# Seven half products in place of eight: Strassen's form in the second MLP product of seven blocks

## The chip, the cores and the metric

The kernel runs on one core of a Trainium2 chip. The metric is the device time in microseconds (us) of one execution. One execution is also taken by the hardware profiler; its span runs from the first to the last instruction. PE or TensorE is the matmul engine (PEld its weight loads), DVE is VectorE, ACT is ScalarE, POOL is GpSimd, SP the queue that issues most DMAs. SBUF is the on-chip memory, PSUM the matmul's accumulators in eight banks.

## The reference

Attention over pooled keys and values, then a residual MLP that first mixes tokens and then channels. 8 batches, 8 heads, 576 tokens of 64 elements a head; model width 512, hidden width 2048.

```python
k_p = k.reshape(B, H, Sp, pool, D).mean(axis=3)        # 576 keys -> 72
v_p = v.reshape(B, H, Sp, pool, D).mean(axis=3)
scores = scale * np.matmul(q, k_p.transpose(0, 1, 3, 2))
attn = softmax(scores)
x = matmul(attn, v_p), heads side by side              # 8 x 576 x 512
a1 = alpha1 * x + beta1
tok = np.einsum('ts,bsd->btd', w_tok, a1)
u = x + lam * tok
a2 = alpha2 * u + beta2
ch = np.maximum(a2 @ w_ch1, 0.0) @ w_ch2
out = u + lam * ch                                     # float32
```

## The kernel before, in words

The 8 x 576 = 4608 rows are cut into 36 chunks of 128 rows (the last 64 rows of two batches share one chunk), and four chunks make a block: nine blocks of 512 rows, 0 to 8. Batch 0's attention and token mix come first. Then the loop at the end of the kernel runs over the blocks n = 0 to 8. In each pass it does block n's MLP and, beside it, the attention and token mix of batch n+1 (so in passes 0 to 6), and it starts the loads of batch n+2.

The order within a pass is written by hand: every step is put in the list `todo` with a number, the list is sorted, and the steps are recorded in that order. The numbers count groups of the MLP: 0 to 15 are the first product's sixteen groups, 16 to 31 the second product's. Each engine and each queue works off its own instructions in the order in which they are recorded, and waits for others by semaphores that the tile layer sets. There is no scheduler behind this.

- First product, `mlp_A(n, j)` (L645): four matmuls of 128x512 give one of 16 groups of hidden columns (L651); ScalarE applies bias and Relu from PSUM to a bf16 tile `Hj` (L657). Its input u_fm is the block's u, times alpha2, in bf16, transposed by DMA (`mix_uT`, L625).
- Second product, `mlp_B(n, m, part)` (L662): for each of four chunks m, 16 matmuls of 128x512 that accumulate in one bank (L686). Then VectorE multiplies the bank by lam (L692), adds it to u (L693), and SP stores the chunk (L695, L699). In block 8 w2 is scaled by lam beforehand (`scale_w2`, L368, four operations), and the last chunk is done in two halves of 256 columns (L675, L680, L682).
- Attention of one batch: `sum_k` (L183, L185) pools keys on GpSimd, `att_K` (L439, L445) transposes them on TensorE, `att_S4` (L511, L518) makes the scores of four heads, ScalarE exponentiates (L540), `att_V` (L479, L481) pools values on VectorE in three operations a pair of heads, `att_AV` (L555, L559) multiplies, and VectorE divides by the row sums: a reciprocal (L561) and x_tm (L563). `att_X` (L577) and `rest_X` (L570) scale x_tm to xs for two heads at a time, on VectorE, or on GpSimd for heads 4 and 5.
- Token mix, `mix_T(b, c)` (L609): five matmuls of 128x512 for each chunk c, from number 21 on, so in the midst of the second product. They need xs of all heads. VectorE adds x (L613) and makes u_bf = u * alpha2 in bf16 (L616); `mix_uT` transposes it into the input of a later block.

Banks: six of the eight are handed out from one pool (`gp`), to whatever asks next; two ("ch") serve the scores and the second product.

Of the kernel before, what the change touches and what calls it, by code (L numbers as in the profile page):

```python
# [7 lines left out]
FP = mybir.dt.float32  # L8
F16 = mybir.dt.float16
BF = mybir.dt.bfloat16  # L10
# [13 lines left out]
def kernel(  # L24
# [176 lines left out]
    b2row = const.tile([4, P], FP, tag="b2row", name="b2row")  # L201
# [18 lines left out]
    nc.scalar.dma_start(out=b2row, in_=moe_beta2.rearrange("(c p) -> c p", p=P))  # L220
    warm = const.tile([P, DM], BF, tag="warm", name="warm")
# [7 lines left out]
    vr16 = const.tile([P, H, 1, D], F16, tag="vr16", name="vr16")  # L229
# [81 lines left out]
    def setup_vectors():  # L311
        ps = gp("ps_vec")
        nc.tensor.transpose(out=ps[:, 0:4], in_=b2row, identity=identity[0:4, 0:4])
        nc.scalar.copy(out=b2c_bf, in_=ps[:, 0:4])
        u_fm[0] = work.tile([P, 4, 2, 258], BF, tag="u_fm", bufs=3, name="u_fm")
        nc.scalar.copy(out=u_fm[0][:, :, 0, 256], in_=ps[:, 0:4])
# [39 lines left out]

    def load_w1(g):
# [8 lines left out]

    def scale_w2(g):
        nc.vector.tensor_tensor(  # L368
            out=w2[g], in0=w2[g], in1=lam_bc.unsqueeze(1).to_broadcast((P, 4, DM)), op=ALU.mult)
# [105 lines left out]
    def att_V(b, hp):  # L475

        t = st1[b]["v"][hp // 2][:, 2 * (hp % 2):2 * (hp % 2) + 2]
        for n in (4, 2):
            nc.vector.tensor_tensor(out=t[:, :, 0:n], in0=t[:, :, 0:n], in1=t[:, :, n:2 * n],  # L479
                                    op=ALU.add)  # L480
        nc.vector.tensor_tensor(out=vp1_pool[hp][:, :, 0:64], in0=t[:, :, 0], in1=t[:, :, 1],  # L481
                                op=ALU.add)
# [101 lines left out]
    st2 = {}  # L584
    u_fm = {}

    def chunk_of(b, c):
        key = (b, c) if c < 4 else (b - b % 2, 4)
        if key not in st2:
            st2[key] = {  # L590
                "u": work.tile([P, DM], FP, tag="u_sb", bufs=12, name="u_sb"),
# [10 lines left out]
    def mix_T(b, c, eng=nc.vector):  # L602
# [13 lines left out]
        eng.tensor_tensor(out=s["u_bf"], in0=s["u"], in1=al2_bc, op=ALU.mult)  # L616
# [19 lines left out]
    Hj = {}  # L636
# [3 lines left out]
    def mlp_A(n, j, t0=0, t1=512):  # L640
# [15 lines left out]
        t = work.tile([P, 512], BF, tag="Hj", bufs=18, name="Hj")  # L656
        nc.scalar.activation(out=t, in_=ps_h, func=AF.Relu, bias=bias_cols[:, j:j + 1], scale=1.0)  # L657
        Hj[n, j] = t
# [3 lines left out]
    def mlp_B(n, m, part):  # L662
# [5 lines left out]
        if n == NBLK - 1 and m == 3:  # L668
            half = part // 2
            cols = slice(256 * half, 256 * half + 256)  # L670
            if part == 2:
                ps_ch[m] = gp("ps_ch2")
            ps = ps_ch[m][:, 0:256]
            for j in range(8 * (part % 2), 8 * (part % 2) + 8):
                nc.tensor.matmul(out=ps, lhsT=Hj[n, j][:, 128 * m:128 * m + 128],  # L675
                                 rhs=w2[j // 4][:, j % 4, cols], start=(j == 0), stop=(j == NJ - 1))
            if part % 2:
                b, c = chunks[4 * n + m]
                u = st2[b, c]["u"][:, cols]
                nc.vector.tensor_tensor(out=u, in0=u, in1=ps, op=ALU.add)  # L680
                for i, queue in enumerate((nc.sync, nc.scalar)):
                    queue.dma_start(out=out[b + i, 512:576, cols], in_=u[64 * i:64 * i + 64, :])  # L682
            return
        ps = ps_ch[m]
        for j in range(4 * part, 4 * part + 4):
            nc.tensor.matmul(out=ps, lhsT=Hj[n, j][:, 128 * m:128 * m + 128], rhs=w2[j // 4][:, j % 4, :],  # L686
                             start=(j == 0), stop=(j == NJ - 1))
        if part == 3:
            b, c = chunks[4 * n + m]
            u = st2[b, c]["u"]  # L690
            if n < NBLK - 1:
                nc.vector.tensor_tensor(out=ps, in0=lam_bc, in1=ps, op=ALU.mult)  # L692
            nc.vector.tensor_tensor(out=u, in0=u, in1=ps, op=ALU.add)  # L693
            if c < 4:
                nc.sync.dma_start(  # L695
                    out=out[b, 0:512, :].rearrange("(p c) d -> p c d", c=4)[:, c, :], in_=u)
# [210 lines left out]
```

## Time and profile before

| what | value |
|---|---|
| time, median of 3 runs | 346.75 us (345.08 to 347.48) |
| span of the profiled execution | 342.9 us |
| the median less this span | 3.85 us |
| granted TensorE clock | 1.000 |
| second product, 128x512 (L686), busy | 128.5 us |
| first product, 128x512 (L651), busy | 124.0 us |
| DMA | 45.76 MB, mean 133 GB/s |

The profiled execution is one execution, and its own time is its span and what lies around it; the table gives the distance to the median. "Busy" is the time in which an engine had such an instruction in hand; matmuls overlap in the array, so the time that one costs in a stream is the distance from one to the next, not its mean duration. Behind the bar of a row stands the idle time of the engine ahead of these instructions and what ended it. In the rows in order of time the first number is the start, the second the length, and in brackets stands the idle time just before.

### The profile page before, as it was taken

What the parts mean: (1) busy time and instruction counts of PE and PEld (TensorE: products, weight loads), DVE (VectorE), ACT (ScalarE), POOL (GpSimd) and SP (SyncE); (2) the same over time, 40 slices, a digit from 0 to 9 for tenths busy, and PEclk for the clock granted to TensorE, in tenths of its full rate; (3) what the DMA queues carried; (4) which work ended last, traced back from release to release, by engine and by line L of the source; (5) the groups of instructions that cost most, each with busy time, mean ns of one, the idle gap of its engine ahead of it and who ended that gap; (6) DMA issues with size and microseconds to landing.
All of it is one profiled execution on the core that took longest, in us unless ns stands there. A gap on an engine that the chain in (4) does not pass through costs nothing.

```text
span 342.9 us, 5845 instructions
## 1 busy us (share of the span) xinstructions
PE 333.6 (97%) x2168; PEld 177.2 (52%) x2204; DVE 222.2 (65%) x477; ACT 146.6 (43%) x277; POOL 94.1 (27%) x110
## 2 busy tenths in 40 slices
PE   8999998999999999999999999999999999999995
PEld 2668753455445544555445544554455445545544
DVE  6772468985777678866866698758676881037511
ACT  3667960079106820484038501870088006604700
POOL 8769357201144022701170217002600200000000
PEclk9999999999999999999999999999999999999999
DMA  8999979959788906894599447982800132011012
GB/s 122 192 222 280 267 133 276 182 140 136 159 228 172 175 0 187 160 227 51 175 161 210 62 127 189 180 130 68 243 35 1 48 77 76 2 61 62 2 54 69
DMA packets 66030, 45.76 MB, mean 133 GB/s; under 512 B 34345, under 2 KB 56237, under 8 KB 66002
## 3 DMA queue, kind: packets, MB, share of 16 engines
q1 hardware_dynamic: 51716, 32.73, 40.6%
q0 software_dynamic: 13824, 12.40, 22.6%
q8 instruction: 17, 0.28, 0.3%
q10 hardware_dynamic: 462, 0.27, 0.3%
q14 instruction: 11, 0.09, 0.1%
HBM read 38.30 MB, written 9.44 MB: 139 GB/s over the span
## 4 chain that ended last, share of the span: by engine, by line
PE 91%; DVE 2%; DMA 2%; POOL 2%; issue 1%; POOLq 0%; DVEq 0%
PE ps_h L651 36%; PE ps_ch L686 34%; PE ps_tok L609 11%; PE ps_s L511 2%; PE ps_av L555 2%; DMA q_bf<-in_q_dram 2%; PE ps_ch L675 1%; PE ps_r L518 1%; PE ps_av L559 1%; PE ps_kp L439 1%; PE ps_w L325 0%; PE ps_q L396 0%; DVE ps_ch L692 0%; DVE u_sb L693 0%; DVE u_sb L613 0%
## 5 line engine op out<-in xcount | busy, mean ns | idle before, releaser
L657 ACT ACTIVATE Hj<-ps_h,bias_cols 128x512 bf16<-128x512 f32 x144 | 98.1, 688 | 165.7 <-PE ps_h L651 164.0
L651 PE MATMUL ps_h<-u_fm,w 128*128 128x512 bf16 (+2 forms) x591 | 132.7, 368 | 1.1 <-DVE bias_cols L654 0.2
L686 PE MATMUL ps_ch<-w,Hj 128*128 128x512 bf16 x543 | 128.5, 379 | 0.9 <-issue 0.5
L651 PEld LDWEIGHTS <-w 128*128 128x128 bf16 x608 | 65.5, 114 | 51.2 <-issue 3.0
L686 PEld LDWEIGHTS <-Hj 128*128 128x128 bf16 x560 | 52.9, 98 | 61.6 <-issue 1.6
L609 PE MATMUL ps_tok<-xs,wtT 128*128 128x512 bf16 (+2 forms) x199 | 44.8, 380 | 1.3 <-DVE xs L577 0.9
L577 POOL TENSOR_TENSOR xs<-x_tm,lamal_bc 128x512 bf16<-128x512 f32 x12 | 15.2, 1267 | 106.1 <-DVE x_tm L563 105.9
L692 DVE TENSOR_TENSOR ps_ch<-lam_bc,ps_ch 128x512 f32<-128x512 f32 x32 | 22.1, 692 | 33.5 <-PE ps_ch L686 33.3
L613 DVE TENSOR_TENSOR u_sb<-x_tm,ps_tok 128x512 f32<-128x512 f32 (+1 forms) x40 | 27.3, 683 | 10.9 <-PE ps_tok L609 10.8
L561 DVE RECIPROCAL rec<-ps_av 128x5 f32<-128x5 f32 x64 | 12.2, 191 | 32.7 <-PE ps_av L559 32.4
L563 DVE TENSOR_TENSOR x_tm<-ps_av,rec 128x320 f32<-128x320 f32 x64 | 31.4, 491 | 2.7
L693 DVE TENSOR_TENSOR u_sb<-u_sb,ps_ch 128x512 f32<-128x512 f32 x35 | 24.0, 687 | 13.6 <-PE ps_ch L686 12.5
L540 ACT ACTIVATE ET<-ps_s 72x512 f16<-72x512 f32 x56 | 32.3, 591 | 0.0
L609 PEld LDWEIGHTS <-wtT 128*128 128x128 bf16 (+3 forms) x200 | 17.3, 100 | 22.1 <-issue 1.7
L616 DVE TENSOR_TENSOR u_bf<-u_sb,al_bc 128x512 bf16<-128x512 f32 x34 | 27.1, 798 | 2.2 <-DMA u_fm<-u_bf 1.1
L479 DVE TENSOR_TENSOR v_u<-v_u 72x512 f32<-72x512 f32 (+1 forms) x48 | 26.4, 550 | 0.8
L183 POOL TENSOR_TENSOR k_raw<-k_raw 128x512 f32<-128x512 f32 x14 | 18.4, 1316 | 10.3 <-DMA k_raw<-in_k_dram 10.2
L555 PEld LDWEIGHTS <-ET 72*128 72x128 f16 x256 | 13.9, 97 | 9.3 <-DVE vp L472 0.6
L185 POOL TENSOR_TENSOR k_bf<-k_raw 128x512 bf16<-128x512 f32 x14 | 18.1, 1295 | 1.1
L79 POOL DMA_DIRECT2D q_bf<-in_q_dram x16 | 12.6, 791 | 15.3 <-DVE v_u L158 14.5
L555 PE MATMUL ps_av<-vp,ET 72*128 72x66 f16 x256 | 15.6, 193 | 0.0
L577 DVE TENSOR_TENSOR xs<-x_tm,lamal_bc 128x512 bf16<-128x512 f32 x20 | 14.7, 736 | 0.7
(130 smaller groups left out, 214.3 us busy)
## 6 DMA issues: line engine op xcount, KB each, us to landing
out_dram<-u_sb SPq DMA_DIRECT2D x32, 256.0 KB
k_raw<-in_k_dram SPq DMA_DIRECT2D x12, 512.0 KB
v_u<-in_v_dram SPq DMA_DIRECT2D x12, 512.0 KB
q_bf<-in_q_dram POOLq DMA_DIRECT2D x16, 256.0 KB, 6.3
w<-in_moe_w_ch_dram POOLq DMA_DIRECT2D x6, 512.0 KB, 13.2
w<-in_moe_w_ch_dram POOLq DMA_DIRECT2D x1, 1024.0 KB, 14.8
k_raw<-in_k_dram POOLq DMA_DIRECT2D x2, 512.0 KB, 16.7
v_main<-in_v_dram POOLq DMA_DIRECT2D x1, 1024.0 KB, 12.0
```

Of the source, the lines that this page charges most:

```text
L479: nc.vector.tensor_tensor(out=t[:, :, 0:n], in0=t[:, :, 0:n], in1=t[:, :, n:2 * n], op=ALU.add)
L540: nc.scalar.activation(out=o, in_=i, func=AF.Exp, bias=0.0, scale=0.125)
L555: nc.tensor.matmul(out=av[:, odd + c, :], lhsT=ET[:, m0:m0 + 128], rhs=vp1[:, hh, :])
L563: nc.vector.tensor_tensor(out=x[:, 1 - odd:6 - odd, dd:dd + D], in0=av[:, :, 0:64], in1=rec.unsqueeze(2).to_broadcast((P, 5, D)), op=ALU.mult)
L577: eng.tensor_tensor(out=xs[:, 0:4, cols], in0=x[:, 1:5, cols], in1=lamal_bc[:, cols].unsqueeze(1).to_broadcast((P, 4, D * (h1 - h0))), op= ...
L609: nc.tensor.matmul(out=ps_tok[p0:p1], lhsT=wtT[0:kk, at, P * c:P * c + p1 - p0], rhs=xs_pool[i][0:kk, sc, :], start=(sc == 0), stop=(sc == 4))
L613: nc.vector.tensor_tensor(out=s["u"][p0:p1, :], in0=x[p0:p1, 1 + c if c < 4 else 5 - 5 * i, :], in1=ps_tok[p0:p1, 0:DM], op=ALU.add)
L616: eng.tensor_tensor(out=s["u_bf"], in0=s["u"], in1=al2_bc, op=ALU.mult)
L651: nc.tensor.matmul(out=ps_h[:, t0:t1 + one], lhsT=w1_of(cc, j), rhs=rhs, start=(cc == 0), stop=(cc == 3))
L657: nc.scalar.activation(out=t, in_=ps_h, func=AF.Relu, bias=bias_cols[:, j:j + 1], scale=1.0)
L686: nc.tensor.matmul(out=ps, lhsT=Hj[n, j][:, 128 * m:128 * m + 128], rhs=w2[j // 4][:, j % 4, :], start=(j == 0), stop=(j == NJ - 1))
L693: nc.vector.tensor_tensor(out=u, in0=u, in1=ps, op=ALU.add)
```

## The change

It replaces the second product of blocks 2 to 8 by a Strassen-Winograd form. Rows, hidden columns and output columns are each halved. The eight products of halves become seven, each done for two chunks of rows (`product(n, i, pp)`): eight matmuls of 128x256 with a weight load each, 112 a block where there were 64 of 128x512. Around them:

- `hidden_sum`: four sums (two calls each) of halves of the hidden tiles, 128x1024 bf16, on VectorE. S2 and S3 go to tiles of their own, two overwrite halves of the hidden tiles.
- `weight_sum`: four sums (two calls each) of halves of w2, once, on VectorE: in pass 1 from number 23.2 on, the last in pass 2.
- `gather`: products that belong together accumulate in one bank; ScalarE copies product 1 to P1, VectorE adds banks to u and product 6 to P1, GpSimd adds P1 to three quarters of u (two in block 8, where VectorE adds the third).
- `stores`: a block's four chunks are stored at its end, after the last gathers.
- w2 is scaled by lam in pass 1, three quarters on VectorE and one on GpSimd; the multiplication by lam remains in block 0 alone. Block 1 has the old product with scaled w2.
- The hidden tiles are four of 128x4x512 in place of 16, and the first product's groups are done in the order 0-3, 8-11, 4-7, 12-15 from block 2 on.

Beside that: alpha2 is multiplied into w_ch1 by ScalarE in pass 0 (`scale_w1`, twelve operations; alpha2 comes in columns by one more small load and the transposing matmul of beta2), so for batches 1 to 7 u_bf is a plain copy, on ScalarE. `att_V` is one tensor_reduce. u lies in one tile a block (three buffers) in place of twelve chunk tiles. Batches 3 to 7 space their token mix by 1.15 in place of 1.3. The constants that the new sums' tiles take over were used only before.

```diff
+    nc.sync.dma_start(out=b2row[4:8], in_=moe_alpha2.rearrange("(c p) -> c p", p=P))
...
+    def scale_w1(i, cc):
+        nc.scalar.activation(out=w1[i][:, cc, :], in_=w1[i][:, cc, :], func=AF.Copy, bias=0.0,
+                             scale=al2_cols[:, cc:cc + 1])
...
-        for n in (4, 2):
-            nc.vector.tensor_tensor(out=t[:, :, 0:n], in0=t[:, :, 0:n], in1=t[:, :, n:2 * n],
-                                    op=ALU.add)
-        nc.vector.tensor_tensor(out=vp1_pool[hp][:, :, 0:64], in0=t[:, :, 0], in1=t[:, :, 1],
-                                op=ALU.add)
+            nc.vector.tensor_reduce(out=vp1_pool[hp][:, :, 0:64],
+                                    in_=t.rearrange("g h p d -> g h d p"), op=ALU.add, axis=AX.X)
...
-        eng.tensor_tensor(out=s["u_bf"], in0=s["u"], in1=al2_bc, op=ALU.mult)
+        if b:
+            nc.scalar.copy(out=s["u_bf"], in_=s["u"])
+        else:
+            eng.tensor_tensor(out=s["u_bf"], in0=s["u"], in1=al2_bc, op=ALU.mult)
...
-            if n < NBLK - 1:
+            if n == 0:
                 nc.vector.tensor_tensor(out=ps, in0=lam_bc, in1=ps, op=ALU.mult)
...
+    def weight_sum(i, g):
+        lo, hi = w2[g], w2[g + 2]
...
+        o, a, b = {
+            1: (T1, lo[:, :, HALF:], lo[:, :, 0:HALF]),
+            3: (T3, hi[:, :, HALF:], lo[:, :, HALF:]),
+            2: (T2, hi[:, :, HALF:], T1),
+            4: (T4, hi[:, :, 0:HALF], T2),
+        }[i]
+        nc.vector.tensor_tensor(out=o, in0=a, in1=b, op=ALU.subtract)
+
+    def hidden_sum(n, i, g):
+        lo, hi, S2, S3 = H4[n, g], H4[n, g + 2], wino["S2"][g], wino["S3"][g]
+        top, low = slice(0, HALF), slice(HALF, DM)
+        o, a, b, op = {
+            3: (S3, lo[:, :, top], lo[:, :, low], ALU.subtract),
+            1: (lo[:, :, low], lo[:, :, low], hi[:, :, low], ALU.add),
+            2: (S2, lo[:, :, low], lo[:, :, top], ALU.subtract),
+            4: (lo[:, :, top], hi[:, :, top], S2, ALU.subtract),
+        }[i]
+        nc.vector.tensor_tensor(out=o, in0=a, in1=b, op=op)
+
+    def product(n, i, pp):
...
+        for j in range(8):
+            nc.tensor.matmul(out=ps, lhsT=stat(j), rhs=moving(j), stop=(j == 7),
+                             start=(i in (1, 5, 6, 7) and (pp == 0 or alone) and j == 0),
+                             skip_group_check=True)
+
+    def gather(n, i):
...
+        if i == 1:
+            wino["P1"] = work.tile([P, 2, HALF], FP, tag="P1", bufs=1, name="P1")
+            nc.scalar.copy(out=wino["P1"], in_=banks[1])
+        elif i == 7:
+            add(nc.vector, low[:, :, R], banks[7])
+        elif i == 2:
+            add(nc.vector, top[:, :, L], banks[1])
...
+        elif i == 5:
+            add(nc.vector, low[:, :, R], banks[5])
+        elif i == 4:
+            add(nc.vector, low[:, :, L], banks[7])
+        elif i == 6:
+            add(nc.vector, wino["P1"], banks[6])
+            add(nc.vector if n == NBLK - 1 else nc.gpsimd, top[:, :, R], wino["P1"])
+            add(nc.gpsimd, low[:, :, R], wino["P1"])
+            add(nc.gpsimd, low[:, :, L], wino["P1"])
+        else:
+            add(nc.vector, top[:, :, R], banks[5])
...
+                at = 8 * (j // 4 % 2) + 4 * (j // 8) + j % 4 if n >= FIRST else j
+                todo.append((at, lambda j=j: mlp_A(n, j)))
...
+        if n == 0:
+            for i in range(3):
+                for cc in range(4):
+                    todo.append((17.3 + 3.4 * i + 0.8 * cc, lambda i=i, cc=cc: scale_w1(i, cc)))
+        if n == FIRST - 1:
+            for g, at, eng in ((0, 3.0, nc.vector), (1, 9.6, nc.vector), (2, 15.0, nc.vector),
+                               (3, 6.8, nc.gpsimd)):
+                todo.append((at, lambda g=g, eng=eng: scale_w2(g, eng)))
+            for s, i in enumerate((1, 3, 2)):
+                for g in range(2):
+                    todo.append((23.2 + 2.6 * s + 1.3 * g, lambda i=i, g=g: weight_sum(i, g)))
+        if n == FIRST:
+            for g in range(2):
+                todo.append((1.2 + g, lambda g=g: weight_sum(4, g)))
+        if n >= FIRST:
+            for i, at in ((3, (4.6, 12.6)), (1, (8.6, 16.6)), (2, (8.8, 16.8)), (4, (18.6, 19.6))):
+                for g in range(2):
+                    todo.append((at[g], lambda i=i, g=g: hidden_sum(n, i, g)))
+            for s, i in enumerate((1, 7, 2, 5, 6, 4, 3)):
+                for pp in range(2):
+                    todo.append((16 + 2 * s + pp, lambda i=i, pp=pp: product(n, i, pp)))
+                todo.append((17.05 + 2 * s, lambda i=i: gather(n, i)))
+            todo.append((29.9, lambda: stores(n, 6)))
+            todo.append((30.0, lambda: stores(n, 3)))
-        if n == NBLK - 1:
-            for g in range(4):
-                todo.append((2.0 + 3.0 * g, lambda g=g: scale_w2(g)))
```

## The prediction

> **What bounds the kernel now.** I read the shares by engine and the chain first, then the groups by form, then the order in time of one block (block 4, 175.5 to 212.0 us), then the end.
>
> ```profile
> PE 333.6 (97%) x2168; PEld 177.2 (52%) x2204; DVE 222.2 (65%) x477; ACT 146.6 (43%) x277; POOL 94.1 (27%) x110
> ...
> PE 91%; DVE 2%; DMA 2%; POOL 2%; issue 1%; POOLq 0%; DVEq 0%
> ```
>
> TensorE is busy 97% and carries 91% of the chain, at clock 1.000: what leaves its queue shortens the kernel, and any wait put in front of it lengthens it at once. The order in time says how much room its waits have:
>
> ```profile
> 191.92 1.03 PE L686 MATMUL ps_ch<-w,Hj 128*128 128x512 bf16 x4
> ...
> 193.14 0.20 DVE L561 RECIPROCAL rec<-ps_av 128x5 f32<-128x5 f32 x1 [2.23 <-PE ps_av L559]
> 193.44 0.49 DVE L563 TENSOR_TENSOR x_tm<-ps_av,rec 128x320 f32<-128x320 f32 x1
> ...
> 194.16 0.20 DVE L561 RECIPROCAL rec<-ps_av 128x5 f32<-128x5 f32 x1 [0.22 <-PE ps_av L559]
> ...
> 194.96 1.26 POOL L577 TENSOR_TENSOR xs<-x_tm,lamal_bc 128x512 bf16<-128x512 f32 x1 [17.32 <-DVE x_tm L563]
> ...
> 195.13 2.54 PE L686 MATMUL ps_ch<-w,Hj 128*128 128x512 bf16 x11
> 195.17 0.20 DVE L561 RECIPROCAL rec<-ps_av 128x5 f32<-128x5 f32 x1 [0.30 <-PE ps_av L559]
> ...
> 196.56 0.75 DVE L577 TENSOR_TENSOR xs<-x_tm,lamal_bc 128x512 bf16<-128x512 f32 x1
> ...
> 197.72 1.24 PE L609 MATMUL ps_tok<-xs,wtT 128*128 128x512 bf16 x5
> ```
>
> The second product starts at 191.92. VectorE turns four attention results into x_tm and ends xs at 197.31; TensorE comes to the token mix, which needs xs, at 197.72. So 0.41 us of slack, and VectorE had only 0.52 us of idle time (0.22 + 0.30) after its first reciprocal. Two other rows decide:
>
> ```profile
> 209.00 1.26 POOL L183 TENSOR_TENSOR k_raw<-k_raw 128x512 f32<-128x512 f32 x1
> 209.20 1.61 DVE L616 TENSOR_TENSOR u_bf<-u_sb,al_bc 128x512 bf16<-128x512 f32 x1
> ```
>
> L616 takes 0.69 alone. Begun under a GpSimd operation it ended 0.55 us after that one's end (210.26). L613 and L692, with an operand in PSUM, keep 0.69 beside GpSimd.
>
> ```profile
> 301.16 10.31 PE ps_ch L686 x47
> ...
> 335.47 3.66 PE L675 MATMUL ps_ch<-w,Hj 128*128 128x256 bf16 x32
> ...
> 339.17 0.42 DVE L680 TENSOR_TENSOR u_sb<-u_sb,ps_ch 128x256 f32<-128x256 f32 x1 [1.33 <-PE ps_ch L675]
> ```
>
> The first line is a run in the chain: the 512-wide matmuls take (10.31 - 0.38)/46 = 0.2158 us apiece, the 256-wide with a weight load each (3.66 - 0.27)/31 = 0.1093.
>
> **The change, part by part.**
>
> (a) Products. In blocks 2 to 8, 64 matmuls of 512 columns (13.81 us) become 7 x 2 x 8 = 112 of 256 (12.24): -1.57 a block, -11.0 in all. Ends: -11.0, and -7.3 if each load cost the 114 ns of L651's strided loads; H4 is read as Hj was, so -11.0.
>
> (b) Sums of H on VectorE, eight a block, 128x1024 in bf16. No row shows one. 128x512 in f32 takes 0.69 and 128x256 takes 0.42, 1.04 ns an element: 1.22 us at that rate. Below, a 16-bit copy of 128x256 takes 0.23, so no sum is under that. Nearest is the 16-bit PSUM copy L403, 128x512 in 0.425, where 128x320 in f32 takes 0.49: half the time per element, so 0.70. The Trainium skill, VectorE: DVE Perf Modes, section on the perf-mode tier table, gives a bf16 tensor_tensor of 2048 elements 1224 ns; by it I estimate 0.69, which no run here shows.
>
> Three of the eight (two at 16.6 and 16.8, one at 18.6 in block units) stand ahead of xs on VectorE. TensorE still reaches the mix 5.83 us after the product starts (48 x 0.1093 + four attention groups of 0.15). VectorE: first x_tm ends at 2.0; two sums to 3.45; second and third heads to 4.76; the third sum would start at 4.8, but GpSimd's xs half (started by the second x_tm, 4.2 to 5.5) has the same conflict as at 209.20, so it ends at 6.03; last head 6.7; xs 7.45; TensorE starts at 7.55: a wait of 1.7 us. Without the conflict 1.15; at 1.22 a sum 3.3; at 0.3 a sum 0.15. I take 1.7, in the five blocks 2 to 6 that carry attention: +8.5. Behind it the gathers (0.69 each, PSUM operand) have 7 to 8 us until their banks are used again. In the first phase VectorE works 12.04 of 16.4 us (block 4) and gets four sums, 2.8 us more: no wait.
>
> (c) Gathers. Scaling w2 beforehand saves 28 x 0.69 us (L692) of VectorE, off the path. GpSimd gets three adds of 1.3 us after product 6, ahead of the next batch's k sums (4 x 1.3, L183 and L185), which ran unhindered until now. Where no fifth chunk lengthens the block (two blocks) the adds end 1.4 us into the next block, the second k sum at 6.8, and TensorE wants it at 6.3 (seven L651 groups and 0.25): 0.6 x 2 = +1.2 (0 to 1.8). Gather 4 stands behind the third add, so VectorE's v sums start about 1 us late; they have 5 us.
>
> (d) Scaling w2 in block 1: three of L368's 2.28 us on VectorE, one on GpSimd. GpSimd's 128x2048 is on no row; L570 64x256 (0.72) to L577 128x512 (1.27) is 2.13 ns an element, 4.5 us (1.3 to 5.3). It stands behind q loads that wait for a VectorE memset after the last v sum, so it starts at about 11.3 us, level with VectorE's second scaling. One waits for the other, then xs of heads 2 and 3 (two SBUF operands) waits until about 18.1. Behind xs stand head 0 and 1, whose bank the last L651 group (due at 16.0) needs: 3.95. The third scaling follows, the mix waits 0.85, and the first scaling delays the first scores 0.4. Sum +5.2; with no conflict 1.5 (the 0.4, and the third scaling ahead of the four heads). I take 5.2: the meeting at 209.20 shows full exclusion. The Trainium skill, SBUF — State Buffer, section "Who interferes with whom", says the pair of ports is held for the whole instruction; the rows confirm that for 1.3 us, and no run here shows it for 4.5. By the rule the term is 5.2, by a wait that ends with one row's length 1.5.
>
> (e) The end. Before, the last matmul ends at 339.13, the last add at 339.59, the span at 342.9: 3.8 us. Now the first add (P1, 0.69) follows product 6, 3.5 us before TensorE's end; two GpSimd adds and one VectorE add of SBUF operands exclude each other (3.2 us); gather 4 (0.69) and two of 0.42 follow, to 2.3 us past TensorE's end. And all four tiles (1 MB) are stored then, not a quarter MB: +2.3 (1.2 to 3.3).
>
> (f) At nothing. Scaling w1: twelve ScalarE operations (about 10 us from L657's 0.69) under ScalarE's 20.5 us gap before 69.62; uncovered, block 1 would start late. The operand copy: 32 x 0.69 leave VectorE, ScalarE (17.8 us gap in every block) takes some 0.6 each; it now waits for u, with only later copies and the next block's first Relu behind it, 3 us on. v in one reduce: 1.39 us becomes about 1.2 (0.7 to 2.3), in the first phase's slack. The new order of the first product's groups moves the same work; the products that read a sum come 3 us or more after it. Weight sums: eight of 0.70 in blocks 1 and 2, second and first phase, under TensorE. Stores at a block's end: on SP's queue the next rem and k loads no longer stand behind a store that waits for u; the stores push v loads about 1 us, needed a block later. One 2 KB load and one ScalarE copy (0.16) in the setup: at most 0.2.
>
> Sum: -11.0 + 8.5 + 1.2 + 5.2 + 2.3 = +6.2. The span of 342.9 becomes 349.1; the median shown (346.75) lies 3.85 above this span, which I add: **353.0 us**.
>
> **Rivals.**
> 1. The conflict does not extend to the new meetings. For it: every such row has f32 operands and 1.3 us at most, and the sums are 16-bit. Against: 209.20. (b) 5 x 1.15, (c) 0.6, (d) 1.5, (e) 1.5: -1.6, 345.1. Chance 0.25.
> 2. Faster: the sums cost 0.3 or less, so xs is late by 0.15. For it: the 0.23 copy. Against: L403. 0.8 + 0 + 1.5 + 1.2 - 11.0 = -7.5, 339.2. It decides once the waits together stay under 7.5 us, a wait of about 0.9 a block with (d) at 1.5. Chance 0.20.
> 3. The sums run at f32's rate: (b) 16.5, total +14.2, 361. Chance 0.06.
> 4. 256-wide products are bound by weight loads at 114 ns: +9.9, 356.7. L675's rows speak against. Chance 0.06.
>
> **The numbers.** My forecast has 0.43, with its own range 350 to 356. The range 339 to 357 holds rivals 1 and 2 and most of 4; it leaves out rival 3 and the tails, some 0.15. About 1% (3.5 us) is what a measurement of this kernel can tell from no change. Slower by over 1%: the forecast, 3 and 4, 0.55; within: rival 1, 0.25; faster: rival 2, 0.20.
>
> **What would show it.** (a) The products' matmuls 0.109 us apart. (b) H sums at 0.70, more beside GpSimd, and in blocks 2 to 6 an idle of TensorE or its loads of about 1.7 us at the mix, released by VectorE's xs. (c) 0.6 us before two of the k products, released by GpSimd. (d) In block 1 TensorE idle for 4 us before its last first-product group, GpSimd's scaling at 4.5 us. (e) Over 5.5 us from the last matmul to the end. No idle at the mix would make the prediction wrong by 8.5, a short GpSimd scaling by 3.7.

## The result, and the profile after

| | before | after |
|---|---|---|
| time, median | 347.12 us (345.08 to 348.61, 4 runs) | 359.89 us (359.28 to 360.60, 4 runs) |
| ratio, 95% interval | | 1.0375 (1.0331 to 1.0419) |
| span of the profiled execution | 342.9 | 357.6 |
| granted TensorE clock | 1.000 | 0.985 |
| TensorE, VectorE busy | 333.6, 222.2 | 329.7, 248.7 |

The kernel is slower, as forecast, but by 12.8 us where the prediction had 6.25, and outside its range. The shares, the clock in forty slices and the chain of the changed kernel:

```profile
PE 329.7 (92%) x2524; PEld 208.3 (58%) x2524; DVE 248.7 (70%) x448; ACT 180.9 (51%) x329; POOL 125.4 (35%) x131
...
PEclk9999999998799999999999999999999999999997
...
PE 65%; DVE 26%; issue 4%; DMA 1%; POOL 1%; ACT 0%; POOLq 0%; DVEq 0%; ACTq 0%
```

TensorE lost 3.9 us of busy time and the span grew by 14.7. VectorE, 2% of the chain before, now carries 26%. The waits of TensorE by what ended them (total us, times, longest):

```profile
PE ps_tok L615 <- DVE xs L579: 8.6, 6, 1.9
PE ps_s L513 <- DVE x_tm L565: 4.2, 1, 4.2
...
PE ps_h L663 <- DVE kp L455: 1.5, 3, 0.5
...
PE ps_kp L443 <- POOL k_bf L185: 1.1, 2, 0.5
```

The first line is the mix (five waits in blocks 2 to 6, and 0.91 us in block 0, which the kernel before has too), the second one place in block 1, the last two are the pooled keys. How long each block took says where the 14.7 us lie. A block is counted from its first matmul of the first product to that of the next block (block 8 to its last matmul's end); "end" is from there to the span's end. All are from one profiled execution each. The last two columns are kernels of the experiments below.

| block | before | after | sums behind xs | late weight sums |
|---|---|---|---|---|
| 1 | 35.21 | 45.12 | 44.43 | 35.21 |
| 2 | 36.49 | 36.82 | 35.11 | 35.05 |
| 3 | 35.22 | 35.81 | 33.78 | 33.62 |
| 4 | 36.49 | 37.99 | 36.56 | 35.05 |
| 5 | 35.21 | 35.82 | 33.77 | 33.62 |
| 6 | 36.49 | 38.00 | 36.60 | 35.04 |
| 7 | 27.63 | 26.04 | 26.04 | 26.04 |
| 8 | 27.83 | 26.21 | 26.20 | 26.21 |
| end | 3.73 | 6.87 | 6.90 | 4.44 |

Block 1 lost 9.9 us, the end 3.1; blocks 2 to 6 lost 4.5 together, 7 and 8 won 1.6 each. What comes before block 1 varies between executions of any kernel here (block 0 began between 26.1 and 30.7 us), so small differences are read from the lengths of blocks, not from spans.

Block 1 can't be read quite alone either. Block 0 took 42.78 us in this execution, and 41.76 before; in runs 1, 3, 4, 6 and 13 below, whose code is the changed kernel's up to there but for the values in run 1, it took 41.70 to 41.78, and in runs 3, 4, 6 and 13 the first scores of block 1 then waited 1.46 or 1.47 us where they waited 0.40 here. VectorE's second scaling began 54.7 or 54.8 us after block 0 did in each of these five executions; what varies is where TensorE waits for it. Blocks 0 and 1 together took 76.97 us before, 87.91 here, and 86.18, 87.03 and 87.88 in runs 4, 5 and 6, which leave the code of both as it is: 9.2 to 10.9 us lost.

Block 1 in order of time:

```profile
80.11 1.55 POOL L79 DMA_DIRECT2D q_bf<-in_q_dram  x2 [16.44 <-DVE v_u L158]
80.80 7.15 DVE L711 TENSOR_TENSOR w<-w,lam_bc 128x2048 bf16<-128x2048 bf16 x1
81.68 4.11 POOL L711 TENSOR_TENSOR w<-w,lam_bc 128x2048 bf16<-128x2048 bf16 x1
...
88.09 0.49 DVE L565 TENSOR_TENSOR x_tm<-ps_av,rec 128x320 f32<-128x320 f32 x1
...
88.63 0.43 PE L513 MATMUL ps_s<-qT,kp 64*72 64x256 bf16 x2 [4.24 <-DVE x_tm L565]
...
89.49 3.57 PE L663 MATMUL ps_h<-u_fm,w 128*128 128x512 bf16 x8
```

VectorE's second scaling (2.28 us alone) met GpSimd's and ended 2.16 us after it, at 87.95. The scores of the last heads waited for the bank that x_tm frees: 4.24 us. Then eight matmuls took 3.57 us where 1.92 is usual. The stretches around it show why (TensorE's busy time first, the granted clock third from the end):

```profile
84.00:88.60 4.60, 0.39 (x6) 0.16 (x6) 4.54 (x3) 0.69 (x1) 1.79 (x1) 0.84 1.36 140
...
90.00:92.00 2.00, 2.00 (x6) 0.61 (x5) 1.93 (x6) 0.69 (x3) 0.00 (x0) 0.50 0.84 154
...
94.00:96.00 2.00, 2.00 (x19) 1.08 (x18) 1.15 (x5) 0.75 (x2) 0.00 (x0) 1.00 1.12 151
```

After the idle the clock was granted at 0.50 until about 93.9, over 5.3 us of work: at most 2.65 us lost by it. The waits of up to 1.9 us at the mix leave the clock at 1.00 in this execution, though not in every one (run 13). The Trainium skill, "TensorE: Matmul & The Clock Gate", Part 1, says that at least one idle window of about 3.4 us halves the clock and that at least about as much sustained work restores it; the idle of 4.24 us and the 5.3 us of work agree, the shorter waits of runs 1 and 13 do not.

The mix of block 4, against the rows of the same place shown before:

```profile
208.71 1.26 POOL L579 TENSOR_TENSOR xs<-x_tm,lamal_bc 128x512 bf16<-128x512 f32 x1 [13.70 <-DVE x_tm L565]
...
209.17 1.35 DVE L746 TENSOR_TENSOR H<-H,h_s 128x1024 bf16<-128x1024 bf16 x1
...
211.19 0.69 DVE L579 TENSOR_TENSOR xs<-x_tm,lamal_bc 128x512 bf16<-128x512 f32 x1
...
212.03 1.24 PE L615 MATMUL ps_tok<-xs,wtT 128*128 128x512 bf16 x5 [1.29 <-DVE xs L579]
```

The third hidden sum, 0.69 alone, ran under GpSimd's half of xs and took 1.35. In blocks 2 to 6 the idle before the mix is 1.36, 1.89, 1.29, 1.89 and 1.28 us. And the end:

```profile
347.04 3.66 PE L775 MATMUL ps_w<-w,H 128*128 128x256 bf16 x32
...
347.96 0.69 DVE L784 TENSOR_TENSOR u_sb<-u_sb,P 128x512 f32<-128x512 f32 x1
348.06 2.94 POOL L784 TENSOR_TENSOR u_sb<-u_sb,P 128x512 f32<-128x512 f32 x2 [22.32 <-issue]
351.03 1.35 DVE L784 TENSOR_TENSOR u_sb<-u_sb,ps_w 128x512 f32<-128x512 f32 x3 [2.38 <-POOL u_sb L784]
...
353.29 1.60 SPq L699 DMA_DIRECT2D out_dram<-u_sb  x3
```

VectorE's last three sums stand behind GpSimd's two, and most of the stores behind those.

### The profile page after: what moved, and what is told of

It is laid out like the page before. It is cut to its first block, busy times and chain, and to the rows that moved or that the text cites. A ratio compares the mean times of both kernels' runs of the same rounds, so it can differ in the third digit from the quotient of the medians.

```text
span 357.6 us, 6496 instructions
## 1 busy us (share of the span) xinstructions
PE 329.7 (92%) x2524; PEld 208.3 (58%) x2524; DVE 248.7 (70%) x448; ACT 180.9 (51%) x329; POOL 125.4 (35%) x131
## 4 chain that ended last, share of the span: by engine, by line
PE 65%; DVE 26%; issue 4%; DMA 1%; POOL 1%; ACT 0%; POOLq 0%; DVEq 0%; ACTq 0%
PE ps_h L663 25%; PE ps_w L775 15%; PE ps_tok L615 11%; PE ps_ch L683 7%; DVE vp L483 6%; DVE x_tm L565 5%; DVE H L746 3%; DVE xs L579 2%; DVE h_s L746 2%; DVE w L711 2%; DVE rec L563 1%; DMA q_bf<-in_q_dram 1%; PE ps_av L557 1%; PE ps_s L513 1%; DVE xs L572 1%
## 5 line engine op out<-in xcount | busy, mean ns | idle before, releaser
L670 ACT ACTIVATE H<-ps_h,bias_cols 128x512 bf16<-128x512 f32 x144 | 98.7, 688 | 57.7 <-PE ps_h L663 56.3
L775 PEld LDWEIGHTS <-H 128*128 128x128 bf16 x560 | 54.2, 98 | 11.0 <-issue 1.2
L623 ACT CAST u_bf<-u_sb 128x512 bf16<-128x512 f32 x32 | 19.8, 618 | 80.4 <-DVE u_sb L619 67.1
L784 POOL TENSOR_TENSOR u_sb<-u_sb,P 128x512 f32<-128x512 f32 x20 | 25.2, 1288 | 91.9 <-DVE P L784 46.0
L615 PE MATMUL ps_tok<-xs,wtT 128*128 128x512 bf16 (+3 forms) x200 | 45.0, 380 | 9.5 <-DVE xs L579 8.6
L775 PE MATMUL ps_w<-w,H 128*128 128x256 bf16 x448 | 53.1, 273 | 0.0
L483 DVE TENSOR_REDUCE vp<-v_u 72x128 f16<-72x1024 f32 x24 | 45.9, 1927 | 0.0
L784 DVE TENSOR_TENSOR u_sb<-u_sb,ps_w 128x512 f32<-128x512 f32 (+1 forms) x37 | 23.6, 656 | 25.1 <-POOL u_sb L784 20.0
L683 PE MATMUL ps_ch<-w,H 128*128 128x512 bf16 x128 | 30.9, 384 | 0.0
L775 PE MATMUL ps_w<-w_t,h_s 128*128 128x256 bf16 x168 | 22.6, 272 | 0.0
L683 PEld LDWEIGHTS <-H 128*128 128x128 bf16 x128 | 12.1, 99 | 14.2 <-issue 1.5
L79 POOL DMA_DIRECT2D q_bf<-in_q_dram x16 | 12.6, 791 | 17.2 <-DVE v_u L158 16.4
```

The source lines that it names most:

```text
L483: nc.vector.tensor_reduce(out=vp1_pool[hp][:, :, 0:64], in_=t.rearrange("g h p d -> g h d p"), op=ALU.add, axis=AX.X)
L615: nc.tensor.matmul(out=ps_tok[p0:p1], lhsT=wtT[0:kk, at, P * c:P * c + p1 - p0], rhs=xs_pool[i][0:kk, sc, :], start=(sc == 0), stop=(sc == 4))
L623: nc.scalar.copy(out=s["u_bf"], in_=s["u"])
L670: nc.scalar.activation(out=H4[n, j // 4][:, j % 4, :], in_=ps_h, func=AF.Relu, bias=bias_cols[:, j:j + 1], scale=1.0)
L683: nc.tensor.matmul(out=ps, lhsT=H_of(n, j)[:, 128 * m:128 * m + 128], rhs=w2[j // 4][:, j % 4, :], start=(j == 0), stop=(j == NJ - 1))
L775: nc.tensor.matmul(out=ps, lhsT=stat(j), rhs=moving(j), stop=(j == 7), start=(i in (1, 5, 6, 7) and (pp == 0 or alone) and j == 0), skip_g ...
```

## The experiments

The theory after the two traces (A): four things cost the time, each by itself: the scaling of w2 in block 1 (with the halved clock, and a reduce that takes 1.93 us where 1.2 was assumed), the sums ahead of xs, GpSimd's adds ahead of the next batch's keys, and the end. The rivals are in the expectations. Times are compared by their ratio to the kernel before, run on the same chip. Runs 5 to 8 were on another chip than runs 1 to 4 and runs 9 to 12 on a third, and one kernel measured on two chips gave ratios 1% apart (run 8); where one run is set against another, the lengths of the blocks are the firmer figure.

**1. The values in three adds again** (the changed kernel with one part undone).

```diff
-            nc.vector.tensor_reduce(out=vp1_pool[hp][:, :, 0:64], ...)
+        for n in (4, 2):
+            nc.vector.tensor_tensor(out=t[:, :, 0:n], in0=t[:, :, 0:n], in1=t[:, :, n:2 * n], ...)
+        nc.vector.tensor_tensor(out=vp1_pool[hp][:, :, 0:64], in0=t[:, :, 0], in1=t[:, :, 1], ...)
```

> The changed kernel with the values pooled as before, in three adds a pair of heads (1.39 us) in place of one reduce (1.93 us). Theory A, the reduce is a cost on the path: in block 1 it makes VectorE 4 x 0.54 = 2.1 us late, so TensorE's idle of 4.24 us ahead of the last scores falls to about 2.1 us, the granted clock stays at 1.00 behind it (it fell to 0.50 for some 4.5 us, worth 3.3 us), and the 0.4 to 0.5 us waits for the kp casts go (0.82 in block 1, about 1 us in blocks 4 and 6): 359.9 - 2.1 - 3.3 - 1.8 = about 352.7. Theory B, the step of the prediction that priced it at nothing: it lies in the slack of the first phase, and the time stays within 1 us of 359.9.

Measured: 365.43 us, 1.0554 (1.0507 to 1.0602). Slower than the changed kernel, so both theories fell. Block 1 was only 1.1 us shorter, blocks 0 and 1 together 2.1 (the idle 3.79, the clock fell as well), and blocks 3 to 6 were 0.9, 2.4, 1.4 and 1.2 us longer. Part of the 2.4 in block 4 is the clock: behind waits of 1.20 and 0.64 us it was granted at 0.50 from 198.1 to 201.5, which costs up to 1.7. The start of block 3 in this kernel:

```profile
152.68 2.09 DVE L483 TENSOR_TENSOR v_u<-v_u 72x512 f32<-72x512 f32 x2
152.76 1.73 POOL L185 TENSOR_TENSOR k_bf<-k_raw 128x512 bf16<-128x512 f32 x1
154.45 1.45 POOL L183 TENSOR_TENSOR k_raw<-k_raw 128x512 f32<-128x512 f32 x1
154.80 1.25 DVE L485 TENSOR_TENSOR vp<-v_u 72x128 f16<-72x128 f32 x1
```

and a block's start in the changed kernel, with the reduce:

```profile
189.12 3.81 DVE L483 TENSOR_REDUCE vp<-v_u 72x128 f16<-72x1024 f32 x2
189.21 1.27 POOL L185 TENSOR_TENSOR k_bf<-k_raw 128x512 bf16<-128x512 f32 x1
190.44 1.27 POOL L183 TENSOR_TENSOR k_raw<-k_raw 128x512 f32<-128x512 f32 x1
```

Three adds take 1.46 us alone and 3.37 beside GpSimd's key sums; the reduce takes 1.9 in either case, and GpSimd's sums beside it keep their 1.27. The reduce, which reads one tensor, escapes the exclusion. So it is long, and yet what keeps the blocks' beginnings on time in this kernel.

**2. The reduce alone** (the kernel before with this part). The edit is that of 1, the other way round.

> The kernel before with this one part of the change: the values pooled in one reduce a pair of heads. Theory A: alone it is hidden in most places, since VectorE has 4.4 us of idle in the first phase of a block (12.04 busy of 16.44); what shows are the kp casts that stand behind a 1.93 us operation, 0.5 us at most of the two casts a block has, six blocks: +1 to +4, 348 to 351, and no idle of TensorE at the mix. Theory C, VectorE is already full: the whole 2.1 us a block in six blocks comes through, 347.1 + 13 = 360.

Measured: 347.45 us, 1.0055 (1.0022 to 1.0087), about +1.9. Blocks 2 and 3 were 0.14 and 1.01 us longer, all others as before, and nothing waited at the mix of blocks 2 to 6. At the lower end of A: in the kernel before, the first phase hides most of it.

**3. Three scalings** (GpSimd's quarter left out).

```diff
-                               (3, 6.8, nc.gpsimd)):
```

> The changed kernel without GpSimd's scaling of the last quarter of w2, which is left out (that quarter is not multiplied by lam); the three on VectorE stay. Theory A, the meeting of the two engines is the cause: VectorE's second scaling takes 2.28 us instead of 7.15, x_tm is 4.87 us earlier, the idle of 4.24 us goes and the granted clock stays at 1.00: 359.9 - 4.24 - 3.3 = about 352.4. Theory D, VectorE has simply too much work in block 1 (four reduces and two scalings ahead of the last scores): the idle stays above 2 us and the time above 356.

Measured: 355.37 us, 1.0260 (1.0233 to 1.0287). Block 1 fell from 45.12 to 38.06, the 4.24 us idle and the halved clock went, VectorE's second scaling took 2.28. So the meeting is worth 7.1 us of block 1 (A), 8.1 with block 0; the other 2.85 us are the amount of VectorE's work (1.47 and 0.42 us waiting for kp), and block 2 got 1.4 us longer, because the weight sums now met GpSimd's key sums. The time fell by 4.0 us by the ratios, where A had 7.5: A's 3.3 for the clock was too much, and block 2 gave 1.4 back.

**4. Sums behind xs.**

```diff
-            for i, at in ((3, (4.6, 12.6)), (1, (8.6, 16.6)), (2, (8.8, 16.8)), (4, (18.6, 19.6))):
+            for i, at in ((3, (4.6, 12.6)), (1, (8.6, 18.85)), (2, (8.8, 18.9)), (4, (21.9, 22.3))):
```

> The changed kernel with the three sums that stood ahead of xs (and the fourth) recorded behind xs. Theory A: the five waits of TensorE at the token mix (1.36, 1.89, 1.29, 1.89, 1.28: 7.71 us) go and nothing takes their place, because the products that read these sums come 2 us or more after the mix begins: 359.9 - 7.7 = about 352.2. Theory E, VectorE's work is only moved: the sums now make product 5 or the sums of the mix late, and at least half comes back as idle of TensorE in the second phase: 356 or more.

Measured: 351.73 us, 1.0162 (1.0113 to 1.0211): 2.1% of 346, about 7.4 us, off the changed kernel. All five waits at the mix are gone, and blocks 2 to 6 are 1.71, 2.03, 1.43, 2.05 and 1.40 us shorter, 8.6 in all. Nothing took their place: A. (The idle shown, 7.71, is smaller than the loss: the profile counts it from the modelled end of the last matmul, which lies some 0.16 us after the place where the next could have been issued.) Blocks 3 and 5 are now 1.44 us shorter than before the change.

**5. One add of P1 on VectorE**, on top of 4.

```diff
-            add(nc.vector if n == NBLK - 1 else nc.gpsimd, top[:, :, R], wino["P1"])
+            add(nc.vector, low[:, :, L], wino["P1"])
+            add(nc.gpsimd, top[:, :, R], wino["P1"])
             add(nc.gpsimd, low[:, :, R], wino["P1"])
-            add(nc.gpsimd, low[:, :, L], wino["P1"])
```

> The kernel with the sums behind xs (351.7) and one of GpSimd's three adds of P1 moved to VectorE. In blocks 4 and 6, where no fifth chunk lengthens the block, that kernel lost 0.54 us before each second k product (GpSimd's k sums late) and about 0.5 us at kp casts. Theory A: the GpSimd adds ahead of the k sums are the cause; 1.3 us less of them ends both waits on GpSimd and lets VectorE's last sums start sooner, so blocks 4 and 6 shorten by 1.0 to 1.5 us each: -2 to -3, about 349. Theory F: the k sums are late because their data or banks are; no change within 0.5 us.

Measured: 349.11 us, 1.0065 (1.0020 to 1.0109). Blocks 4 and 6 fell from 36.56 and 36.60 to 35.04, the waits for k_bf and kp there are gone: A, 3.4 us with the small gains of the other blocks. Before, VectorE had waited up to 3.9 us in its own queue for GpSimd's third add, with the reduces and the kp casts behind it, and TensorE for both. In the changed kernel's block 4:

```profile
187.92 1.29 DVE L784 TENSOR_TENSOR u_sb<-u_sb,ps_w 128x512 f32<-128x512 f32 x2 [3.88 <-POOL u_sb L784]
...
193.57 0.29 PE L443 MATMUL ps_kp<-pool_main,k_bf 128*128 128x64 bf16 x4 [0.54 <-POOL k_bf L185]
...
196.14 1.89 PE L663 MATMUL ps_h<-u_fm,w 128*128 128x512 bf16 x8 [0.54 <-DVE kp L455]
```

**6. The end**, on top of 4: in block 8 all three adds of P1 on VectorE, and each quarter of the output stored as its last sum is recorded, on two queues.

```diff
+            if n == NBLK - 1:
+                for part in (low[:, :, R], low[:, :, L], top[:, :, R]):
+                    add(nc.vector, part, wino["P1"])
+                return
...
+                for at, i in ((21.06, 2), (25.06, 6), (27.06, 4), (30.0, 3)):
+                    todo.append((at, lambda i=i: last_stores(i)))
```

> The kernel with the sums behind xs (351.7), and in block 8 all three adds of P1 on VectorE, no GpSimd, and each quarter of the output stored as soon as its last sum is done. Theory A: the 6.9 us between the last matmul and the end are the two GpSimd adds (2.94 us) that VectorE waits for, and the stores held back to the end; the last sum then ends about 0.5 us after the last matmul and the end comes 3.3 to 4.0 us after it, as before (3.8): -3, about 348.7. Theory G: the end is set by the bytes that are written last; 4 to 5 us remain and the gain is under 2.

Measured: 350.55 us, 1.0100 (1.0049 to 1.0151). The end fell from 6.90 to 4.79 us: 2.1 won, between A and G. GpSimd's adds and the held stores together were two thirds of the surplus over the 3.73 before; the two were not separated, 1.1 us remains, and what holds it was not taken apart. (Block 1, which the edit does not touch, was 1.8 us longer in this profiled execution.)

**7. lam in 16 bits, VectorE alone**, on top of 4. The row lies in a tile that only the warm-up used.

```diff
-            out=w2[g], in0=w2[g], in1=lam_bc.unsqueeze(1).to_broadcast((P, 4, DM)), op=ALU.mult)
+            out=w2[g], in0=w2[g], in1=lam16.unsqueeze(1).to_broadcast((P, 4, DM)), op=ALU.mult)
...
+            todo.append((16.9, lambda: nc.scalar.copy(out=lam16, in_=lam_bc)))
+            for g in range(2):
+                todo.append((30.5 + 0.1 * g, lambda g=g: scale_w2(g, nc.vector)))
...
-            for g, at, eng in ((0, 3.0, nc.vector), (1, 9.6, nc.vector), (2, 15.0, nc.vector),
-                               (3, 6.8, nc.gpsimd)):
+            for g, at in ((2, 12.9), (3, 14.5)):
```

> The kernel with the sums behind xs (351.7), and w2 scaled on VectorE alone, with lam as a 16-bit row (rounded to fp16), two of the four quarters at the end of pass 0 and two in pass 1 ahead of the last scores. Theory A: block 1 loses its 4.3 us idle and the clock stays at 1.00; an operation of 128x2048 with 16-bit operands takes about 1.3 us (the 128x1024 sums take 0.69) instead of 2.28; block 1 falls from 44.4 us to 36 or 37: -8, about 343.5, below the kernel before. Theory H: VectorE has no room for the scaling in these places either, or the mixed 16-bit types run at 2.28 us; then waits of 1 to 3 us appear at the scores or at the mix of block 1, 346 to 348.

Measured: 343.56 us, 0.9886 (0.9844 to 0.9929). Block 1 takes 35.21 us, what it took before the change; block 2 gives 2.0 of the 9.2 us back. A, and already 1.1% faster than before.

**8. All four together.**

> All four corrections together: sums behind xs, one add of P1 on VectorE, the end of block 8, 16-bit scaling of w2 on VectorE. If each is worth what theory A gives it, they add: 351.7 - 2.5 - 3 - 8 = about 338, 2.3 per cent below the kernel before, which is what the products alone save (11.0) less some 3 us. If they compete for VectorE, 341 to 345.

Measured: 337.36 us, 0.9715 (0.9677 to 0.9753); a second time, with other runs of the kernel before, 339.05, 0.9810 (0.9759 to 0.9862):

> The kernel with all four corrections once more, beside the one with late weight sums on the same chip: 0.9715 of before again, and block 2 at 37.5 us.

The 0.9715 was not met again: the two intervals do not touch, so two chips can differ by 1% in this ratio. By the blocks the four add up: blocks 1 to 8 and the end are 21.9 us shorter than in the changed kernel, where runs 4 to 7 won 8.6, 3.4, 2.1 and 7.2. Block 2 is the one left, with 37.5 us both times.

**9. Late weight sums**, on top of 8.

```diff
-            for s, i in enumerate((1, 3, 2)):
+            for s, i in enumerate((1, 3)):
...
-            for g in range(2):
-                todo.append((1.2 + g, lambda g=g: weight_sum(4, g)))
+            for i, at in ((2, 13.65), (4, 22.5)):
+                for g in range(2):
+                    todo.append((at + 0.1 * g, lambda i=i, g=g: weight_sum(i, g)))
```

> The kernel with all four corrections (337.4, 0.9715 of before) with the last four weight sums recorded later: two behind the last attention head of block 2's first product, two in its second product. In that kernel block 2 took 37.52 us where block 3 takes 33.63 and where 35.1 is due: weight sums met GpSimd's k sums (two of them 3.42 us together instead of 1.29) and pushed the kp casts back, 1.17 and 1.01 us of TensorE waiting. Theory A: those 2.2 us go, block 2 takes 35.1 to 35.4: about 335.2. Theory J: in the second product of block 2 there is no room on VectorE and a wait for T2 or T4 appears at products 6 or 4: 336.5 to 338.

Measured: 336.25 us, 0.9727 (0.9686 to 0.9768). Again, beside 8 on the same chip:

> The kernel with late weight sums once more. By the length of block 2 (35.05 against 37.52 us) it should be 2.3 us faster than the kernel with all four corrections on the same chip: a ratio of 0.965 beside 0.9715. If what block 2 gains is lost elsewhere, the two ratios agree within 0.002.

Measured: 337.59 us, 0.9764 (0.9716 to 0.9813). Block 2 takes 35.05 and 35.03 us, no new wait appeared. By the trace 2.5 us are won; the times on one chip differ by 1.5 us and the ratios by 0.005 (0.0065 was expected), inside their intervals, so the gain in time is not shown. This is the version with which to go on: the chain is TensorE's again.

```profile
PE 326.0 (97%) x2524; PEld 209.5 (63%) x2524; DVE 244.0 (73%) x457; ACT 180.5 (54%) x330; POOL 112.4 (34%) x122
...
PE 91%; DMA 3%; POOL 2%; DVE 2%; issue 1%; DVEq 0%; POOLq 0%
```

**10. lam in fp32, same places as in 8.** One line: `in1=lam_bc` again.

> The kernel with all four corrections (337.4), but with lam kept in fp32: the four scalings in the same places on VectorE, at 2.28 us each instead of 1.2. Theory K, the places alone are the cure: the two at the end of pass 0 make the last sums of block 0 2 us late and the two ahead of block 1's mix make xs 2 us late, together +1 to +2.5 us: 338.5 to 340. Theory L, the 16-bit form is the cure: waits at the scores and the mix of block 1 of 3 us or more, and 341 or more.

Measured: 340.97 us, 0.9863 (0.9826 to 0.9900), between K and L by time and K by the trace: block 1 takes 37.93 us, 2.7 longer, with waits of 1.2 us at most. The group of the four scalings here, and in the kernel of 9 with 16-bit lam:

```profile
L711 DVE TENSOR_TENSOR w<-w,lam_bc 128x2048 bf16<-128x2048 bf16 x4 | 9.0, 2280 | 0.0
```

```profile
L713 DVE TENSOR_TENSOR w<-w,early 128x2048 bf16<-128x2048 bf16 x4 | 4.7, 1214 | 0.0
```

Of block 1's 9.9 us the places and the absence of GpSimd won some 7.2, the 16-bit row 2.7. Leaving out GpSimd's quarter alone had won 7.1 (run 3), so that the places win anything by themselves is not shown.

**11. Three adds in the version of 9.** The edit of 1.

> The kernel with all corrections and the late weight sums, with the values pooled in three adds (1.42 us a pair alone) in place of one reduce (1.93 us). Theory M, formed from the first run with three adds, which was 6 us slower than the changed kernel: the adds read two operands in SBUF and wait whenever GpSimd works, the reduce does not (1.91 to 1.94 us beside GpSimd or not); two adds of P1 and four k sums stand at each block's beginning, so the kp casts are late again: +2 to +5 over the kernel with late weight sums. Theory N: with less GpSimd work left the 0.5 us an operation that the adds are shorter shows instead: 0 to -2.

Measured: 341.86 us, 0.9893 (0.9840 to 0.9945): blocks 3 to 6 are 1.4, 1.8, 1.1 and 1.8 us longer, kp late again. M, above its range.

**12. The reduce along rows.**

```diff
-                                    in_=t.rearrange("g h p d -> g h d p"), op=ALU.add, axis=AX.X)
+                                    in_=t, op=ALU.add, axis=AX.X)
```

> The kernel with late weight sums in which the reduce sums along each row of 64 instead of over the eight tokens (the same 1024 fp32 elements read in the order in which they lie, 16 results instead of 128), so that the attention's values are not the reference's; only the duration of the reduce is read. Theory P: the order of reading (a step of 256 bytes from one element to the next) makes the reduce slow, and it falls from 1.93 to about 1.2 us, the rate of the 128x512 rows (0.69). Theory Q: an element of a reduce costs about 1.8 ns whatever the order, and 1.7 us or more remain.

Measured:

```profile
L483 DVE TENSOR_REDUCE vp<-v_u 72x16 f16<-72x1024 f32 x24 | 28.5, 1206 | 0.0
```

1.21 us, as P said: the same 1024 elements took 0.72 us more when each lay 256 bytes from the last. But the edit also makes 16 results of 64 elements out of 128 of eight, so which of the two costs the time, the step between elements or the number of results, is not shown.

**13. A filler in the idle of block 1** (the changed kernel). Run because the 3.3 us of the clock were so far only read from the lengths of the phases.

```diff
+        for i in range(36 if b == 2 and u else 0):
+            nc.tensor.matmul(out=rt[i % 2][:, 256:512], lhsT=warm[:, 0:P], rhs=warm[:, 0:256])
         main(pairs[1][1])
```

> The changed kernel with 36 matmuls of 128x256 on old data (3.9 us at full clock, into unused columns of a scores bank) placed where TensorE was idle for 4.24 us in block 1. What TensorE waits for is not touched. Theory R, the halved clock is a second price on top of the wait: the granted clock stays at 1.00 behind it, the eight matmuls of the last two first-product groups take 1.9 us again instead of 3.57, and block 1 falls by 3.3 us from 45.1 to about 41.8; 359.9 becomes about 356.6 (ratio to before 1.028). Theory S, the slow matmuls come from something else (operands, the weight loads, the meeting of the engines): block 1 stays at 45 us or more.

Measured: 358.19 us, 1.0375 (1.0319 to 1.0431): no change.

```profile
84.86 4.10 PE L530 MATMUL ps_r<-early 128*128 128x256 f16 x36
89.17 0.30 PE L514 MATMUL ps_s<-qT,kp 64*72 64x256 bf16 x2 [0.21 <-DVE x_tm L568]
...
90.97 1.92 PE L666 MATMUL ps_h<-u_fm,w 128*128 128x512 bf16 x7 [1.31 <-DVE x_tm L568]
```

The clock stayed at 1.00 and the matmuls took 1.92 us, so the idle was what halved the clock. But TensorE then ran into the next wait, 1.31 us for the bank that heads 0 and 1 free, and block 1 took 44.13 us: 1.0 us less, not 3.3. With block 0 it was 85.89 us, 2.0 less than in the changed kernel and 0.3 to 2.0 less than in runs 4 to 6, where the clock halved at the same place. So the clock was worth 0.3 to 2.0 us here; VectorE, busy 23.4 of the first 24.0 us of block 1 in the changed kernel and 23.1 here, took the rest back. My sum of 3.3 us fell with this run.

Block 5 was 1.7 us longer in this profiled execution, which hides what was won, and the trace shows why:

```profile
247.44 1.24 PE L618 MATMUL ps_tok<-xs,wtT 128*128 128x512 bf16 x4 [1.88 <-DVE xs L582]
...
249.94 2.34 PE L618 MATMUL ps_tok<-xs,wtT 128*128 128x512 bf16 x5
```

```profile
249.00:251.00 2.00, 2.00 (x9) 1.09 (x8) 1.00 (x2) 0.62 (x1) 0.00 (x0) 0.50 0.04 8
```

Behind a wait of only 1.88 us at the mix the clock was granted at 0.50 from 248.8 to 252.2, and five matmuls of the mix took 2.34 us instead of 1.24. Eight other waits of 1.88 or 1.89 us in these runs left the clock at 1.00; what decides is open. So waits at the mix can cost more than their length.

**14. The scaling alone corrected** (the changed kernel with the edit of 7).

> The changed kernel with only the scaling of w2 corrected (16-bit lam, VectorE alone, two quarters at the end of pass 0); the sums ahead of xs, the three adds on GpSimd and the end stay. Theory A: block 1 takes 35.2 us as before the change, block 2 about 2 us more than the 36.8 it took, and the five waits at the mix stay: -8 from the changed kernel, a ratio to before of about 1.014. Rival: with block 1 no longer late, the k and q loads of the next blocks meet differently and half of the 8 us comes back in blocks 2 and 3: 1.025.

Measured: 353.07 us, 1.0212 (1.0150 to 1.0274). Block 1 takes 35.20 us, block 2 1.3 us more, all others are as in the changed kernel: 8.6 us by the blocks, 1.6% or 5.6 us by the ratios, whose intervals leave about 2.6 us either way. The idle at the mix stays (8.6 us in all). Nothing came back in later blocks beyond block 2's 1.3: A by the blocks, though the ratio lies between A's 1.014 and the rival's 1.025.

## Why the prediction was wrong, step by step

Measured terms: blocks by the table (after, less the run that takes the cause away), in us of span.

| step | predicted | measured | from |
|---|---|---|---|
| (a) products, seven blocks | -11.0 | -10.7 | blocks 2 to 8, late weight sums less before |
| (b) sums ahead of xs | +8.5 | +8.6 | run 4 |
| (c) GpSimd's adds | +1.2 | +3.4 | blocks 2 to 6, run 5 |
| (d) scaling in block 1 | +5.2 | +9.9 | block 1, runs 7 and 14 |
| (e) the end | +2.3 | +3.1 | end, 6.87 less 3.73 |
| (f) and the start | 0 | +0.3 | to the start of block 1: began 0.7 earlier, block 0 took 1.0 longer |
| sum | +6.2 | +14.6 | spans: +14.7 |

The rows are differences of the same lengths of blocks, so that they add up to the span is no proof of any of them; the runs named are.

- (a) Right. The 256-wide products are 0.109 us apart (32 in 3.66 us), rival 4 is out.
- (b) Right in mechanism and size: 0.69 us a sum, 1.35 to 1.43 where it met GpSimd's half of xs, TensorE waiting at the mix in just the five blocks named. Rivals 2 and 3 are out by the 0.69, rival 1 by the 1.35.
- (c) The mechanism was right (0.54 us before the second keys product of blocks 4 and 6, "0.6 x 2"), the size not. The step put the late value sums at nothing, "they have 5 us". They had not: gather 4 waits for GpSimd's third add in VectorE's queue, the reduces behind it take 1.93 us each, and the kp cast between them came late as well (0.54 us in block 4). Run 5 took away 1.5 us in each of the two blocks.
- (d) **The step that failed.** The meeting itself was foreseen: GpSimd took 4.11 us ("4.5"), and TensorE idled for 4.24 ("3.95"), though at the last scores and not before the last first-product group. Two other agreements are luck. The first scores waited 0.40 ("0.4") in this execution alone, and 1.45 to 1.47 in runs 3 to 6 and 13. The 0.87 at the mix ("0.85") did not come from the third scaling, after which VectorE had been idle again (0.48 us at 94.6), but from a small xs operation (0.28 alone) that took 2.39 under a row of GpSimd operations; runs 4, 5 and 13 do not have it.

  What the sum lacked: TensorE's idle in block 1 came to 6.6 us (0.40, 0.42, 4.24, 0.87, and 0.66 for the next block's input), not 5.2, and the halved clock, for which the step has no term, took up to 2.65 more; with some 0.16 for each of the five waits that is about the 9.9 measured. Behind it stands VectorE's load: it was busy for 23.4 of the first 24.0 us of block 1, where it had been for 12.0 of 16.4 before. Without the meeting block 1 was still 2.85 us too long (run 3; the step had 1.5 "with no conflict"), and the meeting cost 7.1 (8.1 with block 0), not 3.7. The step added TensorE's waits as if VectorE caught up between them; when the clock was kept up, TensorE met the next wait for VectorE at once (1.31 us, run 13).
- (e) Right in mechanism, at the upper end of its bounds (1.2 to 3.3): VectorE waited 2.38 us for GpSimd. Run 6 won back 2.1 of the 3.1; the rest is open.
- (f) The reduce at 1.93 was outside the 1.2 taken and inside "0.7 to 2.3"; alone it is nearly hidden (run 2), but not in block 1, where the first scores waited 1.45 to 1.47 us with it in five runs and 0.52 with the adds (run 1). What the point missed is its other side: the adds that it replaces are held up by GpSimd and it is not, which is worth some 6 us in blocks 3 to 6 (5.9 in run 1, up to 1.7 of them the clock's; 6.0 in run 11). The rest of (f), ScalarE's copies (0.62) and scalings, the order of the groups and the stores, shows no wait in the trace.

## What to carry to other kernels

When an edit gives an engine that was off the path new work, sum all that engine's work in the phase first; once it fills the phase, the loss is nearer its surplus than the sum of the waits foreseen on the other engine, and speeding up the other wins only a part (run 13: 0.3 to 2.0 of at most 2.65 us). Work that two engines may not do at the same time is to be placed by engine and by moment: the same change went from 3.75% slower to 2.4 to 2.7% faster by moving sums behind the one thing TensorE was about to need, by keeping GpSimd out of the way, and by a 16-bit row for the scaling. Choose the operation by what it shares as well as by its length: 1.93 us that GpSimd does not hold up beat 1.46 us that it more than doubles.

## What the runs showed of the hardware

- The reduce on VectorE, which reads one tensor, is not held up by GpSimd: it took 1.89 to 1.94 us alone and 1.94 to 1.96 beside GpSimd (changed kernel); three adds of the same data took 1.46 alone and 3.37 beside GpSimd's key sums (run 1).
- The exclusion holds for long operations as well: 2.28 us became 7.15 beside a GpSimd operation of 4.11, and 6.69 in run 1. In both, VectorE's began first (0.88 and 0.42 us ahead) and ended 2.16 and 2.15 us after GpSimd's, so the head start bought next to nothing; why is open. Where GpSimd only issued DMAs (1.56 us at 81.41 in run 3) VectorE's scaling at 82.09 kept its 2.28.
- A reduce of 1024 fp32 elements took 1.21 us as 16 sums of 64 neighbours and 1.93 as 128 sums of eight elements 256 bytes apart; the two causes were not separated.
- A multiplication of 128x2048 in bf16 by a row in fp16 runs at 1.21 us, by a row in fp32 at 2.28. The Trainium skill, "VectorE: DVE Perf Modes", section on the perf-mode tier table, gives a bf16 tensor_tensor of this length 1224 ns; the 1214 measured agree, with the two 16-bit types mixed.
- Idles of 3.79 to 4.25 us were followed each time by a granted clock of 0.50 over 3.4 to 5.8 us of work (changed kernel, runs 1, 4, 5 and 6). Of nine waits of 1.88 or 1.89 us eight left the clock at 1.00 and one was followed by 3.4 us at 0.50 (run 13); so were two waits of 1.20 and 0.64 us close together (run 1). In the long idle, 36 small matmuls on old data kept the clock at 1.00.
